# A fused adaLN, H3 convolution and SwiGLU kernel: a second chunk exchanged by PE transposes, three taps on other engines, modulation rows spread through memory, and a new order

## The chip, the cores and the metric

The kernel runs on one core of a Trainium2 chip. The core has a matrix engine (PE), a vector engine (DVE), a scalar engine (ACT), a general engine (POOL, GpSimd) and a queue (SP) that issues the transfers between device memory (DRAM) and on-chip memory (SBUF, 128 partitions). PE writes to PSUM, from which DVE and ACT read. Each engine works through its own instructions in order and waits on semaphores for the others. The metric is the device time of one execution in microseconds (us); lower is better.

## What is computed

Sequence length S = 2048, width D = 512, FFN width F = 1792, all in float32.

```python
def reference(A_q, A_k, A_v, A_shift_k, A_ssm_k, A_ssm_D, B_x, B_w_gate, B_w_up, B_w_down, c, w_mod):
    def _A_ref(q, k, v, shift_k, ssm_k, ssm_D):
        ...
        for t in range(ks):                                   # ks = 4: short causal convolution of k
            k_shift = k_shift + k_pad[:, t:t + S, :] * shift_k[:, ks - 1 - t][None, None, :]
        kv = k_shift * v
        ...
        y_f = kv_f * kf_f[None, :, :, :]                      # long causal convolution by FFT, per channel
        y = irfft2(y_f, ...)[:, 0, :S, :]
        y = y + kv * ssm_D[None, None, :]
        return q * y
    def _B_ref(x, w_gate, w_up, w_down):
        g = _silu(x @ w_gate)
        u = x @ w_up
        return (g * u) @ w_down
    x = A_q
    mod = (_silu(c) @ w_mod).reshape(c.shape[0], 6, 1, -1)
    sa, ca, ga, sb, cb, gb = (mod[:, 0], mod[:, 1], mod[:, 2], mod[:, 3], mod[:, 4], mod[:, 5])
    h = _layernorm(x, axis=-1) * (1 + ca) + sa
    x = x + ga * _A_ref(h, A_k, A_v, A_shift_k, A_ssm_k, A_ssm_D)
    h = _layernorm(x, axis=-1) * (1 + cb) + sb
    x = x + gb * _B_ref(h, B_w_gate, B_w_up, B_w_down)
    return x
```

## The kernel before

**Two halves.** The first half computes the convolution part (A), the second the FFN (B). The FFN is a loop over 14 blocks of 128 hidden columns and two halves of the tokens, with products by a seven-product scheme (`seventh`) in three passes of a high and a low part each. The change leaves the FFN loop as it is, but for the numbers of the buffers that it takes.

**The convolution** is done for four chunks of 128 channels (`c_` = 0 to 3; `b` in the code of the taps). For each chunk:

1. The short convolution of k with k and v laid channel by partition: `tap0` (line 182) makes `u = k * s0`, `tap` (191) adds `k` shifted by t times `s_t`, for t = 1 to 3, on DVE. `tap2` (200) does the same in two instructions for a half of the columns, a product on ACT and a sum on POOL; no call of it stands in the order of before. `times_v` (209) multiplies a quarter of the columns by v, on DVE or POOL.
2. `x_turn` (224) transposes u v on PE, eight 128x128 blocks a call; ACT copies them out.
3. A long Fourier transform in two steps. First step: `x_first` (252) for X = u v and `k_first` or `kx_first` (260, 256) for the filter K (`SS`, to whose first row `skip` (1050) adds the skip term), PE products with the table `raw`, copied out by ACT. Second step: `x2` (342) for X and `prod` (349) for K, whose evacuation is a DVE multiplication by X's result. `inv` (355) is the inverse of the second step, `y_pe` (495) that of the first. `x2`, `prod` and `inv` have a number n: n // 2 is the chunk, so n = 4 and 5 are the halves of chunk 2.
4. Between the two steps partitions and columns have to be exchanged. For X this is `swap_x` (300), a transpose of 32x32 blocks on DVE, number n // 4 being the chunk: 16 calls before the second step, and 12 to 15 once more for chunk 3 behind the inverse. For K of the chunks 0, 1 and 3 it is done on PE: `k_first` multiplies with the operands exchanged and so gives the transposed block, laid by ACT into `KT`, and `k_turn` (280) transposes it back in another grouping. For K of chunk 2 (`put_k`, `get_k`) and for X of the chunks 0 to 2 behind the inverse (`put`, `get`, 308, 312) it goes out to DRAM and back.
5. `y_gate` (507) multiplies `y` with the gate, which `gate_n` (475, ACT), `gate_m` and `gate_a` (485, 489, POOL unless said) make from the normalised x; `add_y`/`add_c` (517, 1067) add to x and take statistics for the second norm; `do_stats` (1064) takes those of the first, a row block at a time, bn_stats and bn_aggr together.

**The modulation.** `mod_part(i)` (382) multiplies silu(c), spread over 32 columns in `csb`, with vector i of `w_mod`, one quarter of the sum to each group of 32 partitions; `mod_bc(i)` (393) adds the four with a selecting matrix `sel` (128x128) and spreads the result over all partitions, for i = 0, 1, 2, 5, and `mod_T` (402) turns 3 and 4 to a column. `mod_mix` (1059) joins 0, 1 and 2, on which `gate_m` and `gate_a` wait.

**The order is written by hand**: lines 1082 to 1601 are one call a line, and each engine, and SP's queue, issues in that order. Functions under `@parts` (66) are split: the first call issues the PE (or first) part, each further call the evacuation that belongs to it. Buffers are numbered by the strings in `HOMES` (32), one digit a request: `ps` are the four double PSUM banks, the others SBUF slots. A request waits until the last reader of that slot's earlier tile is done.

**The end of the first half**: `inv(6)`, `inv(7)`, `swap_x(12..15)`, the last `y_pe`, `y_gate`, `add_c`, then `do_norm2a`, `norm2b` (525), `norm_t` (542, transposes to `nt`), `norm_s` (550), `op_hi`/`op_lo` (610, 619, the high and low parts `B11` and so on) and the first FFN products `gu_pe` (878, tile `g`), with gate weights split by `w8_hi`/`w8_lo` (690, 695).

Of the kernel before, what the change touches and what calls it, by code (L numbers as in the profile page):

```python
# [78 lines left out]
def adaln_h3_swiglu(ctx, tc, q, kT, vT, shk, ssm, dskip, wgu, wdn, c, wmod, e_fwd, e_inv, w_c, out, out_t):  # L79
# [300 lines left out]

    @parts
# [882 lines left out]
    x2(0, 0)
    load_x(0)
    x2(0, 0)
    tap0(3, dve)
    tap(3, 1)
    do_stats(2, 3)
    x_turn(2, 1)  # L1270
    x2(3, 2)
    x2(3, 2)
    prod(0, 2)
    prod(0, 2)
    do_stats(3, 3)
    prod(0, 0)
    gate_n(2, 0)
    x_first(2, 2)
    x_first(2, 2)
    x_first(2, 3)  # L1280
    x_first(2, 3)
    prod(0, 0)
# [1 line left out]
    x_first(2, 1)
    put_k(2)
    load_v(3)
    x_first(2, 0)
    gate_n(3, 2)
    x_first(2, 0)
    swap_x(5)  # L1290
    tap(3, 2)
# [4 lines left out]
    inv(0)
    tap(3, 3)
    x2(3, 1)
    inv(0)
    x2(3, 1)  # L1300
    inv(0)
    x2(3, 0)
    x2(2, 1)
    x2(2, 1)
    prod(3, 2)
    load_ssm(3)
    x2(2, 0)
    gate_n(3, 1)
    prod(3, 2)
    do_stats(1, 0)  # L1310
    x2(3, 0)
    prod(3, 0)
    prod(3, 0)
    x2(2, 0)
    x2(2, 2)
    put(0)
    get_k(2, 0, 1)
    x2(2, 2)
    prod(3, 1)
    prod(3, 1)  # L1320
    do_stats(1, 3)
    prod(2, 0)
    prod(2, 0)
    prod(2, 1)
# [463 lines left out]
```

## Time and profile before

| | us |
|---|---|
| median of 3 runs | 597.17 (595.6 to 598.14) |
| the profiled execution | 597.2 |
| its span, first to last instruction | 595.2 |
| mean granted PE clock | 0.994 of full |

The profile names tiles as the program does: `s` first step, `kt` and `kvt` transposes of K and of u v, `px`, `pk`, `iv` second step and inverse, `xs` results of `x2`, `pb` modulation, `u` and `vt` the short convolution. Busy times of different engines overlap, and a matmul's end is modelled, so that a PE row also holds some waiting. All instructions are recorded through one helper, so they share a line number and are told apart by their tiles. In the chain of work that ended last, each piece was released by the one in front of it.

### The profile page before, as it was taken

Reading aid. Unit: us, or ns where it says so; the run is one execution under the profiler, and the core shown is the slowest. Engines: PE = TensorE matmul, PEld = TensorE weight load, DVE = VectorE, ACT = ScalarE, POOL = GpSimd, SP = SyncE. Lnnn points to the kernel's source line nnn. Section 1 sums busy time; section 2 is a strip of 40 time slices with the busy share of each in tenths; the row PEclk is TensorE's granted clock in tenths of the full one; section 3 lists DMA queues with packets and bytes.
Section 4 is the critical chain, followed back from the end, with each engine's and each line's share of the span. In section 5 each row is a group of like instructions: output and inputs, shape, how many; then the busy total and the mean of one; then the engine's idle time right before and its main releaser. Section 6 shows DMA issues by size and latency. Waiting matters only on the chain.

```text
span 595.2 us, 10149 instructions
## 1 busy us (share of the span) xinstructions
PE 573.3 (96%) x4054; PEld 444.8 (75%) x4054; DVE 475.2 (80%) x625; ACT 297.2 (50%) x444; POOL 321.8 (54%) x243
## 2 busy tenths in 40 slices
PE   6999899999799999999999999999999999999997
PEld 5874436455687788878888888888888888888885
DVE  5999999998987777877868887865577677777875
ACT  3995769785447443444626445354443333333330
POOL 0312133729131597565867794476283838383991
PEclk9999999999989999999999999999999999999999
DMA  8997969888112189174556462065343434343403
GB/s 289 393 391 263 303 173 289 291 262 336 40 35 107 36 314 385 42 254 171 184 241 230 159 253 101 1 244 213 126 160 123 160 123 160 124 159 124 159 2 141
DMA packets 41329, 112.55 MB, mean 189 GB/s; under 512 B 3121, under 2 KB 19649, under 8 KB 35778
## 3 DMA queue, kind: packets, MB, share of 16 engines
q1 hardware_dynamic: 41282, 111.90, 52.6%
q8 instruction: 32, 0.52, 0.3%
q14 instruction: 15, 0.12, 0.1%
HBM read 73.61 MB, written 38.28 MB: 188 GB/s over the span
## 4 chain that ended last, share of the span: by engine, by line
PE 84%; DVE 10%; ACT 2%; issue 2%; DMA 1%; SPq 0%; ACTq 0%; DVEq 0%
PE dn L63 14%; PE b L63 12%; PE a L63 12%; PE c L63 12%; PE dq L63 10%; PE d L63 6%; PE s L63 4%; DVE X L63 4%; PE px L63 3%; PE g L63 3%; PE pk L63 2%; DVE xs L63 2%; PE y L63 2%; PE iv L63 1%; PE kt L63 1%
## 5 line engine op out<-in xcount | busy, mean ns | idle before, releaser
L63 PE MATMUL dn<-wd,acts 128*128 128x512 f32 x336 | 83.7, 391 | 2.3 <-DVE sg L63 1.5
L63 PE MATMUL b<-op,wsum 128*128 128x512 f32 x312 | 79.3, 389 | 0.0
L63 PEld LDWEIGHTS dn<-wd,acts 128*128 128x128 f32 x336 | 62.8, 188 | 16.6 <-ACT acts L63 2.9
L63 POOL TENSOR_TENSOR wa<-ws,wa 128x512 fp32r<-128x512 f32 (+1 forms) x28 | 35.5, 1291 | 70.5 <-ACT wa L63 70.5
L63 PEld LDWEIGHTS b<-op,wsum 128*128 128x128 f32 x312 | 58.5, 188 | 12.4 <-ACT p L63 0.3
L63 PE MATMUL a<-op,wa 128*128 128x512 f32 x228 | 58.1, 390 | 0.0
L63 PEld LDWEIGHTS a<-op,wa 128*128 128x128 f32 x228 | 42.7, 188 | 8.8
L63 DVE TENSOR_TENSOR x<-x,dn 128x512 f32<-128x512 f32 x56 | 37.0, 678 | 12.6 <-PE dn L63 12.5
L63 DVE STREAM_TRANSPOSE X<-X 128x1024 f32<-128x1024 f32 x20 | 44.9, 2304 | 1.7 <-ACT X L63 1.7
L63 POOL TENSOR_TENSOR acts<-sg,acts 128x512 fp32r<-128x512 f32 x16 | 23.2, 1464 | 40.3 <-ACT acts L63 40.3
L63 ACT ACTIVATE sg<-sg 128x512 f32<-128x512 f32 x20 | 12.6, 632 | 63.9 <-DVE sg L63 63.9
L63 POOL TENSOR_TENSOR vt<-u,vt 128x512 f32<-128x512 f32 x12 | 17.0, 1443 | 46.4 <-DVE u L63 38.0
L63 PE MATMUL c<-op,wa 128*128 128x512 f32 x156 | 39.6, 389 | 0.0
L63 PE MATMUL c<-op,wsum 128*128 128x512 f32 x156 | 39.6, 389 | 0.0
L63 PE MATMUL d<-op,wsum 128*128 128x512 f32 x156 | 39.6, 389 | 0.0
L63 POOL TENSOR_TENSOR s<-s,bcs 128x1024 f32<-128x1024 f32 x12 | 28.5, 2395 | 15.5 <-ACT s L63 15.3
L63 POOL TENSOR_TENSOR wsum<-sr,wsum 128x1024 fp32r<-128x1024 f32 x14 | 35.6, 2540 | 0.0
L63 PEld LDWEIGHTS c<-op,wsum 128*128 128x128 f32 x156 | 29.3, 188 | 6.1
L63 PEld LDWEIGHTS d<-op,wsum 128*128 128x128 f32 x156 | 29.3, 188 | 6.1
L63 PEld LDWEIGHTS c<-op,wa 128*128 128x128 f32 x156 | 29.3, 188 | 6.1
L63 DVE SCALAR_TENSOR_TENSOR u<-kt,shk_sb,u 128x1024 f32<-128x1024 f32 (+6 forms) x15 | 28.7, 1916 | 6.0 <-ACT u L63 5.7
L63 ACT COPY p<-a 128x512 f32<-128x512 f32 x26 | 15.4, 591 | 33.3 <-PE a L63 33.3
(169 smaller groups left out, 1344.3 us busy)
## 6 DMA issues: line engine op xcount, KB each, us to landing
kept<-wsum SPq DMA_DIRECT2D x12, 1024.0 KB, 7.7
wsum<-kept SPq DMA_DIRECT2D x12, 1024.0 KB, 6.7
kept<-wa SPq DMA_DIRECT2D x12, 768.0 KB, 6.8
wa<-kept SPq DMA_DIRECT2D x12, 768.0 KB, 4.3
ws<-in_wgu SPq DMA_DIRECT2D x16, 512.0 KB, 5.9
wm<-in_wmod SPq DMA_DIRECT2D x6, 1024.0 KB, 11.4
away<-X SPq DMA_DIRECT2D x3, 2048.0 KB, 11.0
X<-away SPq DMA_DIRECT2D x3, 2048.0 KB, 7.8
```

Of the source, the lines that this page charges most:

```text
L63: return lambda *a, **k: self.tc.keep_in_program_order(f(*a, **k))
```

## The change

Chunk 2 of X is now exchanged on PE, as K of three chunks is: `xk_first(2, ...)` and `xk_turn(2, ...)` take the place of `x_first(2, ...)` and `swap_x(8)` to `swap_x(11)`. Three taps, (2, 3), (3, 2) and (3, 3), go in halves by `tap2` on ACT and POOL; `tap0(3)` goes to ACT. The vectors 0, 1, 5 and 2 of the modulation are computed together by `mod_rows`, each in its group of 32 partitions, copied out once, written to DRAM and read back to all partitions (`mod_out`, `mod_in`). `do_stats` keeps bn_stats alone, and `do_aggr` takes a tile's four aggregations together. `warm(6)` goes, and the order and the buffer numbers are new throughout.

```diff
-    X, K, KT = {}, {}, {}
+    X, K, KT, XK = {}, {}, {}, {}
...
-    @parts
-    def k_first(c_, jq):
+    def by_columns(T, tag, c_, jq, src, o):
 
         ps = banks("s1")
         for jj in range(4):
             for a in range(2):
                 pe.matmul(
-                    ps[:, a, jj * P : (jj + 1) * P], SS[c_][rows(a), 4 * jq + jj], raw[0][rows(a), 4 * jq + jj],
+                    ps[:, a, jj * P : (jj + 1) * P], src[rows(a), o + jj], raw[0][rows(a), 4 * jq + jj],
                     start=True, stop=True,
                 )
         yield
-        if c_ not in KT:
-            KT[c_] = f16(f"kt{c_}", (P, 4, 32, 32))
+        if c_ not in T:
+            T[c_] = f16(f"{tag}{c_}", (P, 4, 32, 32))
         for a in range(2):
             j = J * a + 4 * jq
             act.copy(
-                KT[c_][:, :, j : j + 4, :].rearrange("p g j k -> p j g k"),
+                T[c_][:, :, j : j + 4, :].rearrange("p g j k -> p j g k"),
                 ps[:, a].rearrange("p (j g k) -> p j g k", j=4, g=4),
             )
 
     @parts
-    def k_turn(c_, m):
+    def k_first(c_, jq):
+        return by_columns(KT, "kt", c_, jq, SS[c_], 4 * jq)
+
+    @parts
+    def xk_first(c_, jq):
+        return by_columns(XK, "xk", c_, jq, XT[c_, jq // 2], 4 * (jq % 2))
+
+    def by_turn(T, tag, half, m):
 
         ps = banks("kt").rearrange("p a (k d) -> p (a k) d", k=4)
-        src = KT[c_].rearrange("p g j k -> p (g j) k")
+        src = half.rearrange("p g j k -> p (g j) k")
         for k in range(8):
             pe.transpose(ps[:, k], src[:, :, 8 * m + k], ident)
         yield
-        if c_ not in K:
-            K[c_] = b16(f"K{c_}")
-        act.copy(K[c_][:, 8 * m : 8 * m + 8, :], ps)
+        if tag not in T:
+            T[tag] = b16(f"T{tag}")
+        act.copy(T[tag][:, 8 * m : 8 * m + 8, :], ps)
+
+    @parts
+    def k_turn(c_, m):
+        return by_turn(K, c_, KT[c_], m)
+
+    @parts
+    def xk_turn(c_, m):
+        return by_turn(X, c_, XK[c_], m)
...
+    ROWS = (0, 1, 5, 2)
+
+    @parts
+    def mod_rows():
+
+        ps = bank("pb")
+        for t in range(4):
+            for k, i in enumerate(ROWS):
+                pe.matmul(ps[32 * k : 32 * k + 32], csb[:, t, :], WM[i][:, t, :], start=(t == 0), stop=(t == 3))
+        yield
+        mv_["rows"] = k2([P, D], F32, "rows")
+        act.copy(mv_["rows"], ps)
+
+    def mod_out():
+        w = mv_["away"] = dp.tile([P, D], F32, tag="modr", name="modr")
+        sp.dma_start(w, mv_.pop("rows"))
+
+    def mod_in():
+        w = mv_["away"].rearrange("(k q) d -> k q d", q=32)
+        sp.dma_start(bcs, w[0:3, 0][None].to_broadcast([P, 3, D]))
+        mv_[0], mv_[1], mv_[2] = bcs[:, 0, :], bcs[:, 1, :], k2([P, D], F32, "ga")
+        sp.dma_start(mv_[2], w[3, 0][None].to_broadcast([P, D]))
+
...
-    @parts
-    def mod_bc(i):
-
-        ps = bank(f"pb{i}")
-        pe.matmul(ps, sel, part.pop(i), start=True, stop=True)
-        yield
-        mv_[i] = k2([P, D], F32, "ga") if i == 2 else bcs[:, min(i, 2), :]
-        act.copy(mv_[i], ps)
-
...
-    sel = cp.tile([P, P], F32, name="sel")
+    sel = cp.tile([P, 1], F32, name="sel")
...
+    def do_stats(t, i):
+        if t not in bnq:
+            bnq[t] = cp.tile([P, TB, 1, 6], F32, name=f"bnq{t}")
+        dve.bn_stats(bnq[t][:, i, 0, :], xt[t][:, i, :])
+
+    bnq = {}
+
     @parts
-    def do_stats(t, i):
-        yield from stats(xt[t], f"a{t}", rows_=[i])
+    def do_aggr(t):
+        for i in range(TB):
+            bn[f"a{t}", i] = bnq[t][:, i]
+        yield from stats(xt[t], f"a{t}", True)
```

The order, cut to the places that are spoken of. The start:

```diff
     load_k(0, 0)
-    warm(6)
     load_shk()
-    tap0(0, act, 0)
-    load_e(2)
+    load_d()
+    load_ssm(0, 0)
+    tap0(0, dve, 0)
+    skip(0)
     tap(0, 1, 0)
     tap(0, 2, 0)
     tap(0, 3, 0)
...
+    load_k(0, 1)
     tap0(0, act, 1)
+    load_e(0)
+    k_first(0, 0)
...
     times_v(0, 0)
     load_v(0, 1)
-    times_v(0, 1, pool)
+    times_v(0, 1)
+    load_v(0, 2)
+    x_turn(0, 0)
+    x_turn(0, 0)
+    k_turn(0, 3)
```

The middle as it stands in the new order:

```python
tap2(2, 3, 1)
prod(0, 0)
prod(0, 0)
silu_c()
tap0(3, act)
prod(0, 1)
tap2(2, 3, 1)
...
inv(1)
prod(0, 2)
swap_x(5)
tap2(2, 3, 0)
silu_c()
inv(0)
swap_x(4)
tap2(2, 3, 0)
times_v(2, 3)
inv(1)
times_v(2, 1)
times_v(2, 2, pool)
times_v(2, 0)
load_x(0)
mod_rows()
tap2(3, 3, 1)
tap2(3, 2, 0)
...
tap(3, 1)
inv(1)
inv(0)
k_turn(1, 1)
k_turn(1, 3)
tap2(3, 2, 1)
tap2(3, 2, 1)
tap2(3, 3, 0)
inv(0)
mod_rows()
tap2(3, 2, 0)
...
x_turn(2, 0)
tap2(3, 3, 0)
swap_x(7)
tap2(3, 3, 1)
...
prod(5, 2)
mod_in()
...
put(1)
get(0)
mod_mix()
```

The end of the first half as it stands in the new order:

```python
do_norm2a(0)
y_pe(1, 2, 3)
mod_T(4)
y_pe(3, 0, 1)
do_norm2a(0)
y_gate(1, 2, 3)
w8_hi(0)
do_norm2a(0)
...
y_pe(2, 0, 1)
...
norm_t(0, 0)
norm_s(0, 0)
add_c(1, 2)
y_gate(1, 0, 1)
add_c(1, 3)
add_c(1, 0)
add_c(1, 1)
op_hi("B11")
op_lo("B11", pool)
y_gate(2, 0, 1)
norm_t(0, 1)
...
y_gate(3, 0, 1)
y_pe(2, 2, 3)
y_pe(3, 2, 3)
next_sbuf()
op_hi("B21")
op_lo("B21")
gu_pe(1, 0, 0)
gu_pe(1, 0, 1)
```

More of the change, by code (lines that the diff above doesn't have):

```diff
@@ L1178, in adaln_h3_swiglu @@
-    skip(1, pool)
-    k_first(1, 0)
+    swap_x(0)
+    times_v(1, 1, pool)
+    x_turn(1, 1)
+    load_wc()
     x_turn(1, 0)
-    x_turn(1, 1)
+    x2(1, 0)
+    x_first(1, 3)
+    x_turn(1, 0)
+    load_v(2)
+    skip(1)
+    tap0(2, dve)
+    tap(2, 1)
+    tap(2, 2)
+    x_first(1, 2)
+    x2(1, 0)
     kx_first(2, 1)
-    k_first(1, 0)
-    load_v(2)
+    x_first(1, 2)
     x_first(1, 0)
+    x_first(1, 0)
+    mod_load(0, 5)
+    load_c()
     x_first(1, 1)
     x_first(1, 1)
-    tap0(2, dve)
@@ L1264, in adaln_h3_swiglu @@
[L1264 to L1282, printed above, removed]
-    do_stats(1, 2)
[L1284 to L1291, printed above, removed]
+    tap2(2, 3, 1)
+    prod(0, 0)
@@ new lines, in adaln_h3_swiglu @@
+    prod(0, 0)
+    silu_c()
+    tap0(3, act)
+    prod(0, 1)
+    tap2(2, 3, 1)
+    prod(0, 1)
+    prod(1, 2)
+    prod(0, 2)
+    prod(1, 2)
+    inv(1)
+    prod(0, 2)
+    swap_x(5)
+    tap2(2, 3, 0)
+    silu_c()
+    inv(0)
+    swap_x(4)
+    tap2(2, 3, 0)
+    times_v(2, 3)
+    inv(1)
+    times_v(2, 1)
+    times_v(2, 2, pool)
+    times_v(2, 0)
+    load_x(0)
+    mod_rows()
+    tap2(3, 3, 1)
+    tap2(3, 2, 0)
+    load_x(2)
+    put_k(2)
+    do_stats(3, 3)
+    tap(3, 1)
+    inv(1)
@@ new lines, in adaln_h3_swiglu @@
+    xk_first(2, 2)
+    do_stats(3, 0)
+    xk_first(2, 1)
+    xk_first(2, 3)
+    xk_first(2, 2)
+    xk_first(2, 3)
+    put(0)
+    do_stats(3, 2)
+    do_stats(0, 1)
+    skip(3, pool)
+    do_aggr(3)
+    xk_first(2, 0)
+    xk_first(2, 1)
+    x2(3, 0)
+    x2(3, 2)
+    xk_first(2, 0)
+    do_aggr(3)
+    x2(3, 0)
+    do_stats(2, 2)
+    get_k(2, 2, 3)
+    mod_out()
+    load_x(1)
+    do_stats(0, 0)
+    times_v(3, 2, pool)
+    prod(3, 0)
+    times_v(3, 0, pool)
+    xk_turn(2, 3)
@@ new lines, in adaln_h3_swiglu @@
+    do_aggr(0)
+    prod(3, 0)
+    times_v(3, 1, pool)
+    x2(3, 2)
+    xk_turn(2, 1)
+    get_k(2, 0, 1)
+    xk_turn(2, 1)
+    xk_turn(2, 2)
+    xk_turn(2, 2)
+    do_aggr(3)
+    xk_turn(2, 0)
+    xk_turn(2, 0)
+    xk_turn(2, 3)
+    x2(2, 2)
+    x2(2, 2)
+    x2(2, 1)
+    prod(2, 2)
+    x2(3, 1)
+    times_v(3, 3, pool)
+    x2(2, 1)
+    x2(3, 1)
+    x2(5, 2)
+    x2(2, 0)
+    x2(5, 2)
+    x2(2, 0)
+    prod(3, 2)
+    prod(3, 1)
+    do_aggr(0)
+    do_aggr(0)
+    gate_n(0, 2)
@@ L1292, in adaln_h3_swiglu @@
+    k_first(3, 0)
+    k_first(3, 0)
+    x2(5, 1)
+    k_first(3, 2)
+    x2(4, 1)
+    x2(5, 1)
+    do_stats(1, 0)
+    do_stats(1, 1)
+    do_stats(1, 2)
+    prod(5, 2)
+    prod(5, 2)
+    mod_in()
+    prod(4, 1)
+    x2(4, 1)
+    prod(4, 1)
+    x2(4, 0)
+    x2(4, 0)
+    gate_n(2, 2)
+    gate_n(0, 1)
+    x2(5, 0)
+    x2(5, 0)
+    put(1)
+    get(0)
+    mod_mix()
+    prod(4, 0)
+    prod(5, 0)
+    prod(4, 0)
+    prod(5, 1)
+    gate_m(0, 0)
     do_stats(1, 3)
-    get_k(2, 2, 3)
@@ L1294, in adaln_h3_swiglu @@
-    x_first(2, 1)
+    x_first(3, 1)
+    prod(5, 1)
     gate_n(3, 0)
[L1296 to L1324, printed above, removed]
@@ L1472, in adaln_h3_swiglu @@
     inv(6)
+    prod(7, 1)
+    put(2)
     inv(6)
-    inv(6)
-    gate_n(1, 3)
-    put(2)
-    prod(7, 1)
+    add_c(0, 0)
+    gate_m(1, 0)
     inv(7)
     mod_load(3, 4)
+    inv(6)
+    inv(7)
     mod_part(3)
+    swap_x(12)
+    get(2)
+    y_pe(0, 2)
+    swap_x(13)
+    inv(7)
+    y_gate(0, 2)
+    gate_a(3, 1)
+    gate_a(1, 0)
+    gate_a(2, 0)
     mod_part(3)
-    inv(7)
-    get(2)
     mod_part(4)
     mod_part(4)
-    mod_bc(5)
-    gate_a(2, 1)
+    mod_T(4)
+    swap_x(15)
```

552 lines of the change are left out of this document (231 added, 321 removed).

## The prediction

> **What bounds the kernel now.** I read the page's first part and its clock slices (tenths of full speed), then the busy time of each engine by stretches, then the chain that ended last. The stretches are mine: 16.7 us is where the first 128x128 transposes of K start (`k_turn(0, ...)`), 136.1 where the inverse transform of the last chunk starts (`inv(6)`), 167.7 the first FFN matmul (`g`), 199.5 the first product of the FFN loop. In each row: length, then busy us (and count) of PE, weight loads, DVE, ACT, POOL, then clock and DMA.
>
> ```profile
> span 595.2 us, 10149 instructions
> PE 573.3 (96%) x4054; PEld 444.8 (75%) x4054; DVE 475.2 (80%) x625; ACT 297.2 (50%) x444; POOL 321.8 (54%) x243
> ...
> PEclk9999999999989999999999999999999999999999
> ...
> 16.70:136.10 119.40, 114.78 (x1734) 68.31 (x1734) 116.63 (x113) 96.61 (x117) 40.88 (x26) 1.00 0.90 296
> 136.10:167.70 31.60, 27.80 (x379) 20.55 (x371) 29.51 (x58) 15.76 (x21) 17.40 (x10) 0.90 0.42 167
> 167.70:199.50 31.80, 29.98 (x139) 24.38 (x138) 23.81 (x25) 16.14 (x23) 11.38 (x11) 1.00 0.19 67
> 199.50:595.20 395.70, 391.14 (x1738) 322.67 (x1737) 295.71 (x418) 161.08 (x273) 250.73 (x192) 1.00 0.44 164
> ```
>
> From 199.5 us on PE is busy 391 of 396 us, and the change touches nothing there but buffer numbers: no gain. In the first stretch DVE is busy 116.6 of 119.4 us, so 2.8 us idle, and PE 114.8. PE's figure flatters it, since a matmul that waits is shown as running. Its own pace stands in pieces of the chain without waits and in the groups:
>
> ```profile
> 18.76 0.96 PE kvt L63 x8
> 19.72 0.90 PE kt L63 x8
> ...
> 22.48 10.03 PE s L63 x176
> ...
> L63 PE MATMUL kt<-ident,kt 128*128 128x128 f32 x96 | 12.6, 281 | 2.0 <-ACT kt L63 1.3 <-DVE xs L63 0.6
> L63 PE MATMUL kvt<-ident,vt 128*128 128x128 f32 x64 | 9.3, 291 | 0.4 <-POOL vt L63 0.4
> L63 PE MATMUL pb<-wm,csb 128*32 128x512 f32 x48 | 5.9, 600 | 0.0
> L63 PE MATMUL pb<-part,sel 128*128 128x512 f32 x8 | 4.0, 606 | 0.0
> ```
>
> So 57 ns for a small matmul (10.03/176), 112 for a transpose of K (0.90/8), 120 for one of V, 123 for `pb` from `wm` and 500 for `pb` from `part`. Of the 1734 instructions 96 are `kt`, 64 `kvt`, 32 `wm` (four of six vectors), 6 `part` (three of four), 1536 the rest: 10.8 + 7.7 + 3.9 + 3.0 + 87.6 = **113.0 us of PE work in 119.4**. PE really waits 6.4 us, and the chain shows for whom:
>
> ```profile
> 63.52 2.23 DVE X L63
> 65.75 0.14 issue
> 65.88 1.09 PE px L63 x16
> ...
> 101.06 2.31 DVE X L63
> 103.37 0.14 issue
> 103.50 1.95 PE px L63 x32
> ```
>
> `px` (the forward product) starts when DVE's 32x32 transposes of X end. So in this stretch DVE is the bound and PE stands 6.4 us behind it: whatever leaves DVE, the gain there ends at about 6 us.
>
> **The change part by part.** Durations:
>
> ```profile
> L63 DVE STREAM_TRANSPOSE X<-X 128x1024 f32<-128x1024 f32 x20 | 44.9, 2304 | 1.7 <-ACT X L63 1.7
> L63 DVE SCALAR_TENSOR_TENSOR u<-kt,shk_sb,u 128x2045 f32<-128x2045 f32 x3 | 7.0, 2328 | 0.0
> L63 DVE TENSOR_SCALAR u<-kt,shk_sb 128x2048 f32<-128x2048 f32 x3 | 4.4, 1457 | 0.4 <-DMA kt<-in_kT 0.4
> L63 DVE TENSOR_TENSOR vt<-u,vt 128x512 f32<-128x512 f32 x4 | 3.7, 956 | 0.1
> L63 ACT ACTIVATE u<-kt,shk_sb 128x1024 f32<-128x1024 f32 x2 | 2.3, 1148 | 2.8 <-DMA kt<-in_kT 2.8
> L63 ACT COPY X<-s 128x1024 f32<-128x1024 f32 x16 | 15.4, 1030 | 0.5 <-PE s L63 0.4
> L63 ACT COPY kt<-s 128x512 f32<-128x512 f32 x24 | 12.5, 637 | 2.0 <-PE s L63 2.0
> L63 ACT COPY K<-kt 128x1024 f32<-128x1024 f32 x12 | 12.0, 1024 | 2.2 <-PE kt L63 2.1
> L63 ACT COPY part<-pb 128x512 f32<-128x512 f32 x6 | 3.5, 590 | 4.5 <-PE pb L63 4.5
> L63 POOL TENSOR_TENSOR s<-s,bcs 128x1024 f32<-128x1024 f32 x12 | 28.5, 2395 | 15.5 <-ACT s L63 15.3
> L63 POOL TENSOR_TENSOR vt<-u,vt 128x512 f32<-128x512 f32 x12 | 17.0, 1443 | 46.4 <-DVE u L63 38.0 <-DVE ss L63 8.5
> ```
>
> *DVE, first stretch.* Four exchanges `swap_x(8..11)` go: 4 x 44.9/20 = -9.0. Three taps of 2046 or 2045 columns go: -7.0. `tap0(3)` goes to ACT: -1.5. Two more `times_v` stand on DVE: +1.9; `skip(1)` +0.3. `add_c(0, 0)` moves behind `inv(6)`: -1.6 here, back in the tail. Together -16.9: **DVE 99.7 us**.
>
> *PE.* `xk_turn(2, ...)` adds 32 transposes: 4 x 0.90 = +3.6. `xk_first` issues as many matmuls as `x_first`, with the operands exchanged: 0. `mod_rows` issues the 32 instructions of four `mod_part`: 0. Three `mod_bc` in the stretch go: 6 x 0.5 = -3.0. **PE 113.6 us.** `warm(6)` lies in time in which PE waits for data: 0; the clock is full in the first slices with it; were it half without, matmuls that wait for loads anyway would take double until 15 us.
>
> *ACT.* Six half taps at 1.15 (+6.9), `tap0(3)` at twice that (+2.3), four `xk_turn` copies (+4.0), `xk_first` copies 4 x (2 x 0.52 - 0.96) = +0.3; copies of `part` and, of the same shape, of the broadcasts, 7 x 0.6, go and one `rows` comes (-3.6). **96.6 + 9.9 = 106.5 us**: not the bound, but near it.
>
> *POOL.* Six adds of 128x1024: the trace has that shape as `s<-s,bcs`, 2.4 each, so +14.4; two `times_v` fewer, -2.9; `skip(1)` -0.5; one `w8_lo` from the tail, +2.4: 54 of 119 us. New waits there: `times_v(2, 2)` and so the transposes of V behind the adds of chunk 2; in the new order they stand some 6 us of PE work ahead of `x_turn(2, 0)`. The adds of chunk 3 stand 25 us ahead of theirs. 0; if that cover went, PE would wait for up to one add, 2.4.
>
> *The memory broadcast.* `mod_out` and `mod_in` put three transfers in SP's queue: 0.25 MB out, 0.75 and 0.25 MB back to all partitions. The nearest row, from issue to landing:
>
> ```profile
> rs<-rs SPq DMA_DIRECT2D x4, 256.0 KB, 4.7
> ```
>
> Out and back one after the other, with twice that for the larger one: 10 to 15 us from the copy of the rows to the vectors. Between that copy and `mod_mix`, which needs them, stand over 25 us of DVE and 35 of PE work: 0. On SP's queue `mod_in` stands ahead of `put(1)`, `get(0)`, `get(1)`; `put(1)` waits for `inv(2)` much longer. Without the cover, `mod_mix` would hold DVE, and behind it the `prod` that PE's banks wait for: 5 to 10 us.
>
> *The start.* The first tap moves to DVE; the first loads are in another order.
>
> ```profile
> 11.95 3.91 DVE L63 SCALAR_TENSOR_TENSOR u<-kt,shk_sb,u 128x1024 f32<-128x1024 f32 x3
> ...
> 16.70 2.06 PE L63 MATMUL kt<-ident,kt 128*128 128x128 f32 x16 [1.27 <-ACT kt L63]
> ```
>
> These three taps of the second half of chunk 0 end at 15.9 now. DVE's own half tap (1.46/2) is 0.4 shorter than ACT's 1.15 that they wait for, and some 0.3 of waiting between goes (an estimate), so they end at about 15.2; then two `times_v` (2 x 0.93) come ahead of PE's first transposes, which are V's now: 17.0 for 16.7, +0.3, bounds -1 and +2.
>
> *First stretch, sum.* If PE never waited: 17.0 + 113.6 = 130.6 for 136.1, a gain of 5.5. As bound, DVE was idle 2.8 of 119.4 (2.3%). I give PE the same share: 113.6/0.977 = 116.3, so 133.3: **-2.8**, bounds -5.5 and 0.
>
> *The tail* is a chain: `inv(6)`, ACT's copies, four transposes on DVE, `y`, statistics of x, normalising, transposes `nt`, `g`.
>
> ```profile
> 140.08 6.68 DVE L63 STREAM_TRANSPOSE X<-X 128x1024 f32<-128x1024 f32 x3 [1.75 <-ACT X L63]
> ...
> 153.96 0.17 DVE L63 TENSOR_SCALAR rsb<-mvb 128x4 f32<-128x4 f32 x1
> ...
> 164.08 3.68 PE L63 MATMUL y<-X,ei 128*64 128x128 f32 x32 [1.54 <-ACT hraw L63]
> ...
> 165.00:166.00 1.00, 1.00 (x12) 1.00 (x12) 1.00 (x2) 0.90 (x1) 0.46 (x1) 0.50 0.44 168
> ```
>
> Up to the statistics it is the same instructions, 17.9 us from `inv(6)`. Behind that, the last `y` ran at a clock of 0.50, 32 in 3.68 us, between PE's gaps. The new order leaves two `y` behind `nt` instead of one, the last when DVE has freed its bank (`add_c(1, ...)` and two `y_gate`: some 10 us behind the statistics, 27.9 from `inv(6)`), but `g` starts with a half that needs only `B11` and weights that POOL has split long before. So 27.9 + 1.9 (full clock) to 3.7 (half): 29.8 to 31.6, for 31.6 now: **-0.9**, bounds -1.8 and +1.8 (both `y` at half clock).
>
> *167.7 to 199.5*: PE has 30 of 31.8 us of the same work in a new order: 0, bounds +-1.
>
> Sum: -2.8 - 0.9 = -3.7. The profiled execution took 597.2 (span 595.2 and 2.0 around it), and the median of the runs shown is 597.17, the same: **593.5 us**.
>
> **The rivals.** *PE packs fully* (-5.5 - 1.8): 589.9. For it: the 176 matmuls from 22.5 to 32.5 us show 10 us of PE without a wait even now. Against: ACT at 106.5 now feeds every bank.
>
> *The wait changes its owner.* ACT and PE stand within 7 us of each other and each waits for the other's banks, as PE and DVE do now; if PE keeps waiting 6.4 us, 17.0 + 113.6 + 6.4 = 137.0, and with the tail 597.2. For it: ACT's half taps of chunks 2 and 3 (six, 6.9 us) and `tap0(3)` lie within some 15 us in which PE has inverse transforms and transposes to be copied; against it: ACT still has 10 us of slack.
>
> *Slower: POOL's adds hold DVE.* A DVE instruction with two operands in SBUF that starts beside one of POOL waits for it:
>
> ```profile
> 117.41 4.76 POOL L63 TENSOR_TENSOR s<-s,bcs 128x1024 f32<-128x1024 f32 x2
> ...
> L63 DVE TENSOR_TENSOR s<-s,bcs x4: 1210/1210/3162, 120.1 to 125.5; 128x1024 f32<-128x1024 f32 x4
> ```
>
> The first of the four started at 120.10, POOL's second ended at 122.17, and it took 3.16 for 1.21. Six adds could hold DVE 6 x 2.4 = 14.4 us. DVE has that slack against PE, so a hold costs only where `prod` and PE's banks are queued behind it; it decides when over 5.5 + 0.9 + 3 = 9.4 us of the 14.4 fall there. With all of them PE ends at 130.6 + 14.4 = 145.0: 597.2 + 8.9 - 0.9 = 605. Against: beside the adds the new order has transposes, `prod` (one operand in PSUM) and statistics on DVE, which do not show this. [...]
>
> **How the numbers follow.** Chances: the forecast (591 to 595) 0.50, full packing 0.10, the wait's new owner (595 to 599) 0.30, slower by POOL 0.10 (600 to 605). A measurement of this kernel tells about 0.5% (3.0 us) from no change: faster is below 594.2. Of the forecast 0.47 lies there, with packing 0.57; slower 0.10; the rest, 0.33, within. The range of 589.5 to 598 leaves out 0.04 below and 0.13 above.
>
> **What would show it.** Right: `inv(6)` starts near 133, DVE's busy time up to there near 100, PE's near 114; ACT near 106. Wrong: `px` or `kvt` waiting for ACT or POOL in the table of waits; a DVE instruction of two SBUF operands over 3 us between 45 and 70 us; `mod_mix` or `put` waiting for the broadcast; PE's first transposes after 18 us; a clock of 0.50 for over 7 us in front of `g`.

## The result and the profile after

The changed kernel takes **590.33 us** (median of 5 runs, 589.25 to 592.59) against 597.17 (595.6 to 598.48, now 5 runs): ratio 0.9897, 95% interval 0.9865 to 0.993, 1.0% faster. The forecast was 593.5, in a range of 589.5 to 598. The profiled execution took 592.16 us, so the traces show 5.0 of the 6.8 us between the medians. The five spans lie between 587.5 and 590.8 us, at mean granted clocks between 0.994 and 1.000. Larger samples of the kernel before, taken with the experiments (11 to 21 runs), have medians of 595.6 to 596.9 us, by which the gain is 5.3 to 6.6 us.

The first lines of the changed kernel's page:

```profile
span 590.4 us, 10177 instructions
...
PE 568.6 (96%) x4066; PEld 444.4 (75%) x4066; DVE 456.9 (77%) x621; ACT 304.6 (52%) x451; POOL 330.6 (56%) x246
```

PE is as full as before, in a span 4.8 us shorter; DVE has lost 18 us and ACT and POOL have gained 7 and 9. Where the 4.8 us lie is seen when the trace is cut at the prediction's marks: first transposes, `inv(6)`, first `g`, first product of the loop. The rows by stretches of the changed kernel (length, then busy us and count of PE, weight loads, DVE, ACT, POOL, then clock and DMA); the two below cut the first stretch at 77 us, and the last two show the clock in the tail:

```profile
17.09:133.47 116.38, 114.70 (x1760) 71.54 (x1760) 98.17 (x103) 106.58 (x129) 51.21 (x30) 1.00 0.97 321
133.47:164.54 31.07, 26.58 (x376) 19.69 (x368) 28.54 (x61) 13.90 (x17) 16.14 (x8) 0.95 0.43 167
164.54:194.05 29.51, 29.46 (x138) 24.22 (x137) 24.03 (x26) 17.08 (x24) 9.87 (x10) 1.00 0.14 54
...
49.00:77.00 28.00, 27.27 (x360) 17.19 (x345) 27.85 (x35) 26.42 (x32) 18.49 (x12) 1.00 0.84 279
77.00:133.50 56.50, 56.47 (x942) 29.59 (x941) 42.31 (x52) 51.20 (x62) 25.81 (x14) 1.00 1.01 301
...
142.00:146.00 4.00, 3.30 (x28) 2.39 (x22) 4.00 (x3) 0.58 (x1) 3.20 (x2) 0.92 0.51 150
146.00:150.00 4.00, 3.93 (x48) 3.69 (x44) 2.32 (x7) 0.00 (x0) 0.00 (x0) 0.66 1.01 404
```

And of the kernel before, the first stretch from 49 us on, cut at 77 us too, and the hand-over from the first `g` to the loop, cut at the exact starts:

```profile
49.00:77.00 28.00, 25.36 (x328) 14.34 (x332) 27.62 (x34) 19.96 (x24) 6.37 (x5) 1.00 0.80 243
77.00:136.12 59.12, 57.14 (x939) 29.10 (x923) 58.23 (x59) 47.50 (x58) 27.16 (x15) 1.00 0.89 268
...
167.69:199.32 31.63, 29.80 (x138) 24.21 (x137) 23.64 (x25) 16.16 (x23) 11.30 (x11) 1.00 0.19 67
```

The same cuts for all kernels that were run (from the start of each mark's first matmul; the loop is the span less the start of its first product). The last two columns are the time lost to a granted clock of 0.50 in the first stretch and the tail: the sum of length x (1 - clock) over rows of 2 or 4 us, or over the stretch where its loss is under 4 us. So 1.7 us lost are 3.4 us at half clock; a stretch becomes longer by the loss only where PE sets its pace:

| kernel | start | first stretch | tail | hand-over | loop | lost, first | lost, tail |
|---|---|---|---|---|---|---|---|
| before | 16.70 | 119.42 | 31.57 | 31.63 | 395.9 | 0 | 3.4 |
| changed | 17.09 | 116.38 | 31.07 | 29.51 | 396.4 | 0 | 1.7 |
| `e1_swap2` | 16.30 | 122.77 | 30.67 | 29.48 | 396.2 | 3.4 | 0 |
| `e2_taps_dve` | 16.74 | 125.39 | 30.12 | 29.49 | 395.9 | 1.7 | 0 |
| `e3_both` | 16.52 | 130.69 | 29.39 | 29.53 | 396.1 | 6.8 | 0 |
| `e4_after_dve` | 16.24 | 125.66 | 30.32 | 29.48 | 396.2 | 5.1 | 0 |
| `e5_before_dve` | 15.79 | 131.90 | 31.70 | 31.54 | 395.9 | 6.8 | 3.5 |
| `e6_after_pe` | 16.45 | 118.40 | 33.25 | 29.56 | 396.2 | 0 | 5.1 |
| `e7_before_pe` | 16.47 | 119.67 | 30.70 | 31.67 | 395.9 | 0 | 1.5 |
| `e8_before_sg` | 17.45 | 119.78 | 30.76 | 30.92 | 395.9 | 0 | 1.5 |
| `e9_after_dve_late` | 16.05 | 119.68 | 32.53 | 29.51 | 396.2 | 0 | 3.4 |
| `e10_after_ends` | 15.76 | 115.51 | 34.94 | 29.48 | 396.4 | 0 | 5.1 |
| `e11_before_tap0` | 16.14 | 125.81 | 30.70 | 31.51 | 395.9 | 1.7 | 1.8 |
| `e12_after_ends2` | 16.38 | 115.51 | 32.77 | 30.67 | 396.3 | 0 | 5.1 |

So the change gave, in the trace: start +0.4, first stretch -3.0, tail -0.5, hand-over -2.1, loop +0.5; sum -4.8. How much of that is scatter between executions, the table shows. Seven kernels have the start of the changed one (`changed`, `e1` to `e4`, `e6`, `e9`) and reach the first transposes at 16.05 to 17.09 us, so +0.4 says nothing. Five have the tail of the kernel before (`before`, `e5`, `e7`, `e8`, `e11`): it takes 30.70 to 30.76 us where 1.5 to 1.8 us are lost by the clock, and 31.57 and 31.70 where 3.4 and 3.5 are. The changed kernel, with 1.7 us lost, takes 31.07: its -0.5 is one spell of half clock less, which comes and goes in the old order too, and a gain of the new tail is not shown. The first stretch and the hand-over do repeat: kernels of the old order whose first stretch was left alone (`e7` but for PE's added work, `e8`) have 119.67 and 119.78 us for 119.42, and the hand-over is 31.5 to 31.7 in the old order but for `e8`, which changes it, and 29.5 to 29.6 in the new but for `e12`.

Two things are to be seen in the rows. DVE has 18 us of slack over the first stretch (98.2 of 116.4), but none of it from 49 to 77 us: there it is busy 27.85 of 28.00 us. PE gains all the same: before, it was idle 2.6 us from 49 to 77 us and 2.0 behind 77; now it is idle 0.7 and nothing. And the hand-over holds no wait of PE any more: 29.46 busy of 29.51, where before 1.83 us were missing.

Timeline rows of the changed kernel (start, length, engine, operation; in brackets the idle time before and what ended it), from the start, the first stretch, the tail and the hand-over:

```profile
8.32 0.28 DVE L63 TENSOR_TENSOR ss<-ss,bcs 1x128 f32<-1x128 f32 x1 [2.60 <-DMA ss<-in_ssm]
16.30 2.37 DVE L63 TENSOR_TENSOR vt<-u,vt 128x512 f32<-128x512 f32 x2
16.35 3.45 POOL L63 TENSOR_TENSOR vt<-u,vt 128x512 f32<-128x512 f32 x2 [15.04 <-DVE u L63]
18.73 0.75 PE L63 MATMUL kvt<-ident,vt 128*128 128x128 f32 x4 [0.91 <-DVE vt L63]
...
55.81 1.06 DVE L63 COPY csb<-csil 128x128 f32<-128x128 f32 x1
...
75.88 1.04 DVE L63 SCALAR_TENSOR_TENSOR rsa<-mva,rsa 128x4 f32<-128x4 f32 x1
76.01 2.06 PE L63 MATMUL kt<-ident,xk 128*128 128x128 f32 x16 [0.62 <-DVE xs L63]
...
108.17 4.54 DVE L63 TENSOR_TENSOR s<-s,bcs 128x1024 f32<-128x1024 f32 x2
...
140.80 1.09 PE L63 MATMUL y<-T,ei 128*64 128x128 f32 x16 [0.93 <-DMA T<-away]
141.83 1.07 PE L63 MATMUL pb<-wm,csb 128*32 128x512 f32 x8
142.95 0.33 SPq L63 DMA_DIRECT2D ei<-in_e_inv  x1
145.55 4.38 PE L63 MATMUL y<-X,ei 128*64 128x128 f32 x48
...
188.25 5.97 PE L63 MATMUL dn<-wd,acts 128*128 128x512 f32 x24
```

DVE waits 2.6 us for a load in the middle of the first taps. Its two `vt` stand beside POOL's and take 2.37 us where 2 x 0.93 was reckoned (the same pair took 2.36 in the kernel before), and two sums at 108 us, beside POOL's, 4.54 for 2 x 1.21. Two small operations from 49 to 77 us are long too: the copy to `csb` took 0.18 us in the kernel before, and the operation on `rsa` 0.15 there at 69.18 us, both where POOL was idle. They stand beside POOL's add of 54.79 to 56.79 us and its products from 74.33 us on, so some 1.8 of the 27.85 us (1.06 - 0.18 and 1.04 - 0.15) are likely time in which DVE was held, an estimate from these times. The load of the second table `ei` is issued when the last product of the modulation weights ends (141.83 + 1.07). The last row is the hand-over: 24 `dn` in one run, where the kernel before stopped behind six:

```profile
195.16 4.33 PE L63 MATMUL dn<-wd,acts 128*128 128x512 f32 x18 [1.47 <-DVE sg L63]
```

### The profile page after: what moved, and what is told of

The parts are those of the page before. It is cut to its first block, busy times and chain, and to the rows that moved or that the text cites. A ratio compares the mean times of both kernels' runs of the same rounds, so it can differ in the third digit from the quotient of the medians.

```text
span 590.4 us, 10177 instructions
## 1 busy us (share of the span) xinstructions
PE 568.6 (96%) x4066; PEld 444.4 (75%) x4066; DVE 456.9 (77%) x621; ACT 304.6 (52%) x451; POOL 330.6 (56%) x246
## 4 chain that ended last, share of the span: by engine, by line
PE 84%; DVE 7%; DMA 5%; ACT 2%; issue 1%; SPq 0%; DVEq 0%; ACTq 0%
PE dn L63 15%; PE b L63 12%; PE a L63 12%; PE c L63 12%; PE dq L63 10%; PE d L63 6%; PE s L63 4%; PE g L63 4%; PE px L63 2%; PE pk L63 2%; DMA T<-away 2%; DMA away<-T 2%; PE y L63 2%; DVE u L63 1%; PE nt L63 1%
## 5 line engine op out<-in xcount | busy, mean ns | idle before, releaser
L63 POOL TENSOR_TENSOR wa<-ws,wa 128x512 fp32r<-128x512 f32 (+1 forms) x28 | 34.2, 1243 | 58.3 <-ACT wa L63 58.3
L63 POOL TENSOR_TENSOR s<-s,bcs 128x1024 f32<-128x1024 f32 x12 | 29.9, 2513 | 27.1 <-ACT s L63 26.0
L63 DVE STREAM_TRANSPOSE X<-X 128x1024 f32<-128x1024 f32 x16 | 36.3, 2315 | 2.2 <-ACT X L63 2.2
L63 DVE TENSOR_TENSOR xs<-pk,xs 128x1024 f32<-128x1024 f32 x24 | 28.3, 1215 | 11.5 <-PE pk L63 11.2
L63 DVE TENSOR_TENSOR acc<-acc,dq 128x512 f32<-128x512 f32 x40 | 26.7, 683 | 6.8 <-PE dq L63 6.8
L63 ACT COPY p<-a 128x512 f32<-128x512 f32 x26 | 15.4, 590 | 31.7 <-PE a L63 31.7
```

The costliest lines, as they stand in the source:

```text
L63: return lambda *a, **k: self.tc.keep_in_program_order(f(*a, **k))
```

## The experiments

Each expectation names the theory that was held when it was written; the first one, with the result just seen, was that the sums of work per engine over the whole first stretch decide.

**Parts of the change undone.** The changed kernel with the exchange of X's chunk 2 back on DVE, with the taps back on DVE, and with both; the order of the calls that stay is that of the changed kernel.

```diff
-    xk_first(2, 2)
+    x_first(2, 2)
...
-    xk_turn(2, 1)
-    xk_turn(2, 2)
-    xk_turn(2, 2)
+    swap_x(11)
+    swap_x(10)
```

> The changed kernel with chunk 2 of X exchanged on DVE again (x_first and swap_x(8..11)), all else as changed: DVE 98.4 + 9.0 = 107.4, PE 113.6 - 3.6 = 110.0, ACT 106.8 - 4.3 = 102.5. Bound theory (a stretch costs about its most loaded engine): PE is still the most loaded and lighter, so -2 to +1.5 us: 588.5 to 592. Rival (the exchange on PE is where the gain comes from): +3 or more, 593.5 upwards.

```diff
-    tap2(2, 3, 0)
+    tap(2, 3)
...
-    tap0(3, act)
+    tap0(3, dve)
...
-    tap2(3, 2, 0)
+    tap(3, 2)
...
-    tap2(3, 3, 1)
+    tap(3, 3)
```

> The changed kernel with the three taps and tap0(3) back on DVE: DVE 98.4 + 8.5 = 106.9, ACT 106.8 - 9.1 = 97.7, POOL 51.4 - 14 = 37. Bound theory: PE 113.6 stays the bound, 0 to +2 us: 590 to 592.5. Rival (the taps on ACT and POOL are where the gain comes from): +3 or more. Third (POOL's adds hold DVE): faster, -1 to -3.

> The changed kernel with both back on DVE, in the new order and with the new modulation: DVE 98.4 + 9.0 + 8.5 = 115.9, PE 110.0. Bound theory: DVE is the bound again, the first stretch 2 to 4 us longer: 592.5 to 594.5, inv(6) at 135.5 to 137.5. Rival (the new order carries the gain): within 1 us of the changed kernel.

Measured: 597.49 us, ratio to before 1.0032 (1.001 to 1.0054); 599.11 us, 1.0047 (1.0024 to 1.0069); 604.33 us, 1.0159 (1.0118 to 1.02). Set against the changed kernel's 0.9897 that is 1.35%, 1.50% and 2.62% of 597 us: in the new order the exchange is worth 8.1 us, the taps 9.0, both 15.6. My theory, that only the sums of the engines over the stretch count, fell in all three. Timeline rows of the first and one of the second:

```profile
79.40 1.95 PE L62 MATMUL px<-X,wc 64*32 64x512 f32 x32 [1.75 <-DVE X L62]
...
87.46 1.96 PE L62 MATMUL pk<-T,wc 64*32 64x512 f32 x16 [3.54 <-DVE xs L62]
```

```profile
76.68 3.50 PE L62 MATMUL px<-X,wc 64*32 64x512 f32 x32 [4.62 <-DVE X L62]
```

PE waits again for DVE, as in the kernel before: in the second kernel 4.62 us for transposes of X, in the first 1.75 us for them and then 3.54 for an `xs`, the multiplication that frees PE's bank, which stands behind the four transposes that came back. So the stretch in which DVE sets the pace reaches to 87 us there. A part of these prices is the clock, which fell to 0.50 inside such waits: at 87.4 us in the one of 3.54, at 76.5 in the one of 4.62, and in the third kernel at 74.6 and 95.1 in waits of 4.60 and 4.02 us. So 3.4, 1.7 and 6.8 us are lost in the three first stretches, where the changed kernel loses none. The third kernel's row by stretch, to be read beside the first row of the changed kernel:

```profile
16.52:147.21 130.69, 117.48 (x1728) 69.49 (x1728) 114.44 (x111) 95.24 (x113) 38.64 (x24) 0.95 0.86 287
```

It has 2.2 us less on DVE than the kernel before, and its first stretch is 11.3 us longer than there, at a mean clock of 0.95 (6.8 us lost). So the new order (with the modulation by rows, which stays) is no gain by itself: with DVE's old work in it the kernel is 1.6% slower than before, although it keeps the shorter hand-over. The likely reason is that the order is made for a DVE that is free at certain places; it was not taken apart further.

**Load added** (these four ran first). Sixteen statistics of the first norm made twice (10.9 us more on DVE), and 32 transposes of K's chunk 1 made twice (3.6 us more on PE), each in the kernel before and in the changed one; results stay the same.

```diff
+                if name[0] == "a":
+                    dve.bn_stats(bn[name, i][:, 0, :], xs[:, i, :])
```

> The kernel before with each of the 16 bn_stats of the first norm issued twice into the same place: 16 x 0.68 = 10.9 us more on DVE, nothing else. Bound theory (before, DVE sets the first stretch): DVE 116.6 + 10.9 in a stretch of 119.4, so at least +8 us: 605 (603 to 609), inv(6) at 144 to 147 instead of 136.1. Rival (the order of the work and its waits set the time, not DVE's load): both this and the same edit on the changed kernel cost alike, some 3 to 6 us.

```diff
+        dve.bn_stats(bnq[t][:, i, 0, :], xt[t][:, i, :])
```

> The changed kernel with the same edit, 16 bn_stats more (10.9 us of DVE). Bound theory: DVE 98.4 + 10.9 = 109.3 stays under PE's 113.6, so 0 to +3 us: 590 to 594, inv(6) at 133.5 to 136. Rival: as much as on the kernel before.

```diff
-            pe.transpose(ps[:, k], src[:, :, 8 * m + k], ident)
+            for _ in range(2 if c_ == 1 else 1):
+                pe.transpose(ps[:, k], src[:, :, 8 * m + k], ident)
```

> The kernel before with the 32 transposes of K's chunk 1 issued twice: 32 x 0.112 = 3.6 us more on PE. Bound theory: PE waits 6.4 us for DVE in that stretch, so 0 to +1.5 us: 597 to 598.7. Rival (PE sets the stretch already, as its 96% of busy time says): +3.6.

```diff
-            pe.transpose(ps[:, k], src[:, :, 8 * m + k], ident)
+            for _ in range(2 if T is K and tag == 1 else 1):
+                pe.transpose(ps[:, k], src[:, :, 8 * m + k], ident)
```

> The changed kernel with the same 32 transposes more (3.6 us of PE). Bound theory: PE is the bound now, so +2.5 to +4 us: 593 to 594.3, inv(6) at 136 to 137.5. Rival: as on the kernel before, or nothing.

Measured: DVE's load makes the kernel before 607.82 us (1.0191, 1.0145 to 1.0236) and the changed one 599.69 (1.0068, 1.0034 to 1.0102), 9.4 us over 590.33. PE's load makes the kernel before 596.62 (1.0003, 0.9984 to 1.0022), nothing, and the changed one 593.64 (0.9953, 0.9928 to 0.9977), 3.3 us more, though the intervals of the two just touch. PE's half is as expected in the kernel before: 3.6 us of PE work lie in time in which PE waits (first stretch +0.25 us). In the changed kernel the total is as expected, but `inv(6)` came at 134.85 us for 136 to 137.5: 2.0 of the 3.6 us count in the first stretch. The tail, in which no transpose was added, is 2.2 us longer and loses 3.4 us more by the clock, and that varies between executions: four of the ten runs took 590.6 to 591.8 us at mean clocks of 0.998 to 1.000, five 594.1 to 595.7 at 0.990 to 0.994. So the price of that PE work seems nearer 2 than 3.3 us. DVE's load on the kernel before is as expected in the time; of the 12.5 us by which its first stretch is longer, up to 6.8 are lost by the clock. On the changed kernel DVE's load is a miss: it should hardly have felt it. Its trace says where:

```profile
81.17 3.68 PE L63 MATMUL kt<-ident,xk 128*128 128x128 f32 x16 [6.70 <-DVE xs L63]
```

Ten of the sixteen stand ahead of that `xs`, 10 x 0.68 = 6.8 us, and PE waits 6.70 us, where it waited 0.62 in the changed kernel. The six behind it cost little. So a new theory, in place of the sums, which the undone parts had refuted as well: not the sum, but DVE's chain from 49 to 77 us.

**Where the load stands.** If that is so, load behind 77 us should be free: the last six statistics made three times, 8.2 us. And its counterpart in the kernel before: 4.4 us taken from DVE in the old order.

```diff
-        dve.bn_stats(bnq[t][:, i, 0, :], xt[t][:, i, :])
+        for _ in range(3 if t == 1 or (t, i) in ((2, 0), (2, 1)) else 1):
+            dve.bn_stats(bnq[t][:, i, 0, :], xt[t][:, i, :])
```

> The changed kernel with the last six statistics of the first norm (those that stand behind 77 us) made three times instead of once: 12 more instructions of about 0.68 us, 8.2 us more on DVE, all behind the stretch from 49 to 77 us. Only DVE's time is changed, no result. Theory now (DVE is at its limit only from 49 to 77 us, and idle 18 us in the rest of the first stretch): inv(6) no more than 1 us later than 133.5, 590 to 592.5. Rival (DVE's whole sum of the first stretch counts, as the 10.9 us of the run with all 16 doubled seemed to say at 0.85 us each): 597 to 598.

```diff
-    tap0(1, dve)
+    tap0(1, act)
...
-    tap0(2, dve)
+    tap0(2, act)
...
-    tap0(3, dve)
+    tap0(3, act)
```

> The kernel before with the first tap of chunks 1, 2 and 3 on ACT instead of DVE, order and all else unchanged: DVE 4.4 us less, ACT 6.9 us more. Theory (in the kernel before DVE sets the first stretch, and PE has 6 us to give): inv(6) 3 to 4.4 us earlier than 136.1, 592.5 to 594.5. Rival (work taken from DVE gains only where DVE's chain is, or ACT's copies for PE come later by as much): 596 to 598.

Measured: 595.43 us (0.9972, 0.9954 to 0.999), and 601.27 (1.0079, 1.0059 to 1.01). The first lies between the theories: its first stretch is 3.3 us longer, for 8.2 us of load, though DVE had 14 us of slack behind 77 us. Timeline rows of PE and DVE:

```profile
86.38 1.09 PE L63 MATMUL iv<-xs,wc 32*64 32x512 f32 x8 [0.52 <-DVE xs L63]
...
100.92 2.51 DVE L63 TENSOR_TENSOR xs<-pk,xs 128x1024 f32<-128x1024 f32 x2 [4.87 <-PE pk L63]
...
109.00 1.16 PE L63 MATMUL s<-er,ss 64*128 64x128 f32 x16 [1.06 <-DVE xs L63]
```

The slack could not be moved: a statistic queued in front of an `xs` held PE, 0.52 us at 86 and 1.06 at 109 us, though DVE idled 4.87 us between the two. The second run is the plainest case. DVE has less to do, and the kernel is 4.4 us slower. Timeline rows of ACT, DVE and PE:

```profile
19.93 2.00 ACT L63 ACTIVATE u<-kt,shk_sb 128x2048 f32<-128x2048 f32 x1 [2.33 <-DMA kt<-in_kT]
...
21.97 7.12 DVE L63 SCALAR_TENSOR_TENSOR u<-kt,shk_sb,u 128x2047 f32<-128x2047 f32 x3 [3.45 <-ACT u L63]
...
22.89 1.98 PE L63 MATMUL kvt<-ident,vt 128*128 128x128 f32 x8 [2.83 <-ACT K L63]
```

On ACT the first tap waits 2.33 us for its load, and ACT's copies for PE stand in the queue behind it. So PE stops, and the taps on DVE stop too. Its first stretch is 6.4 us longer than in the kernel before, with 3.2 us less on DVE; up to 1.7 of the 6.4 are half clock, from 22.2 us on, inside the stop, to 25.6.

**The hand-over.** In the kernel before, the product that the last `dn` wait for is put ahead of other work on DVE.

```diff
+    gu_act(1, 1)
     gu_end(0, 1)
...
-    gu_act(1, 1)
```

> The kernel before with one line moved at the hand-over to the FFN loop: DVE's product of gu_act(1, 1) stands ahead of gu_end(0, 1) and the first downs(1) instead of behind them, so that dn's second bank comes free earlier. If the wait of 1.47 us of dn for DVE sg is the lost time there: 167.7 to the loop 31.6 -> 30.3, time 595.9 for 597.2. If the time there hangs on another thing (the splits, the load of wa): no change.

Measured: 594.82 us (0.9991, 0.9971 to 1.001), no difference by the whole time. The stretch itself can be read, since the loop is the same to 0.1 us in the kernels of the old order:

```profile
167.99:198.91 30.92, 29.77 (x139) 24.18 (x138) 24.40 (x25) 16.96 (x24) 11.45 (x10) 1.00 0.20 69
```

30.92 for 31.63: 0.7 of the 2.1 us of the hand-over come with that one step; the wait has changed from DVE's 1.47 us to ACT's:

```profile
181.37 11.21 PE L63 MATMUL g<-op,wg 128*128 128x512 f32 x48 [0.36 <-ACT hraw L63]
...
194.74 4.33 PE L63 MATMUL dn<-wd,acts 128*128 128x512 f32 x18 [0.79 <-ACT acts L63]
```

The rest (that 0.79, the 0.36 for ACT's `hraw`, and 0.3 us in PE's busy time) goes with the other steps of the new order; which of them was not taken apart.

**A better version tried.** The changed kernel with its start put right (the wait of 2.60 us) and its tail in another order. First version:

```diff
-    skip(0)
     tap(0, 1, 0)
     tap(0, 2, 0)
     tap(0, 3, 0)
+    skip(0)
     load_k(0, 1)
-    tap0(0, act, 1)
+    tap0(0, dve, 1)
...
     put(2)
...
+    get(2)
     mod_load(3, 4)
...
+    y_pe(1, 0, 1)
...
     y_pe(0, 2)
...
     mod_part(3)
     mod_part(4)
...
     y_pe(0, 3)
```

> The changed kernel with both ends of its first part put in another order: at the start skip(0) behind the first half taps and tap0(0) of the second half on DVE; in the tail get(2) ahead of the two loads of the modulation weights, y_pe(1, 0, 1) and y_pe(0, 2) ahead of mod_part, y_gate(0, 2) behind the last exchanges. Theory (DVE's wait for the load of ss and ACT's table load hold the start, 32 products y at half clock ahead of y_pe(0, 3) hold the statistics): first transposes 1 to 1.5 us earlier than 17.1, inv(6) to g 29 to 30 us for 31.1, total 587 to 588.5. Rival at the start (the loads set the pace of the first 35 us, whatever the order): no gain there. Rival in the tail (DVE's four exchanges and the loads set it): 31 us as now; both rivals: 590 to 591.

Second version: the start as in the first, `get(2)` behind `mod_load(3, 4)` again, and

```diff
     mod_part(3)
...
+    mod_part(4)
...
+    load_einv2()
+    y_pe(1, 0, 1)
+    y_pe(0, 2)
```

> The changed kernel with the start of the run before last kept (skip(0) behind the first half taps, tap0(0) of the second half on DVE), and another tail: both mod_part right behind inv(7), so that load_einv2, which takes their weights' place, is issued some 2 us earlier than 142.95, and only then y_pe(1, 0, 1) and y_pe(0, 2); mod_load and get(2) in the order of the changed kernel. Theory (y_pe(0, 3) waits for that load, and the load for mod_part(4)): inv(6) at 131.3 as in the run with the first version, inv(6) to g 29 to 30 us for 31.1, total 586.5 to 588. Rival (the loads of these 20 us together set the tail, whatever their order): 31 us, total 588.5 to 590. If the start too gave nothing: 590.

Measured: 594.79 us (0.9976, 0.9958 to 0.9993) and 591.84 (0.9928, 0.9909 to 0.9946). Neither is faster than the changed kernel. The first stretch is 0.9 us shorter in both, and PE's wait of 0.91 us for `vt` at its head is gone. `inv(6)` starts at 131.27 and 131.89 us for 133.47; the other 1.3 and 0.7 are an earlier start, but the start as it was scatters from 16.05 to 17.09 us, so of these (15.76 and 16.38) little is shown to be the new order. The tail gave it back. Rows of the first version's tail, and its clock:

```profile
131.27:166.21 34.94, 28.79 (x376) 22.43 (x368) 28.72 (x61) 14.02 (x17) 16.11 (x8) 0.85 0.46 175
...
146.00:150.00 4.00, 2.96 (x21) 2.66 (x22) 1.13 (x4) 0.00 (x0) 0.00 (x0) 0.51 1.00 398
150.00:154.00 4.00, 4.00 (x35) 3.98 (x37) 2.06 (x11) 1.05 (x1) 1.02 (x1) 0.50 0.04 13
154.00:158.00 4.00, 4.00 (x56) 4.00 (x56) 3.43 (x8) 2.13 (x4) 0.00 (x0) 0.71 0.01 2
```

```profile
147.04 1.97 PE L62 MATMUL y<-X,ei 128*64 128x128 f32 x16 [4.15 <-DMA ei<-in_e_inv]
```

I had taken the cover from a load: `y_pe(0, 3)` needs the second table, the table is asked for only behind `mod_part(4)`, and the 32 products that I moved ahead had covered its way. Timeline rows of the second version, two of the tail and one of the hand-over:

```profile
139.21 0.33 SPq L62 DMA_DIRECT2D ei<-in_e_inv  x1
144.70 1.47 PE L62 MATMUL y<-X,ei 128*64 128x128 f32 x16 [1.80 <-DVE X L62]
...
191.12 4.37 PE L62 MATMUL dn<-wd,acts 128*128 128x512 f32 x18 [1.25 <-DVE x L62]
```

Here the load is asked for 3.7 us earlier and is in time, and DVE's transposes set the pace; but PE stands idle 1.80 us for them, its clock is at half for 10 us in all behind that (5.1 us lost for 1.7 in the changed kernel), and at the hand-over a wait for DVE is back. Its tail loses 3.4 us more by the clock than the changed kernel's; taken off in full that would leave 29.4 us, as expected, but this is an estimate and was not measured.

## Why the prediction came out as it did

**The first stretch: right in size, the reason only half right.** Forecast -2.8 with `inv(6)` at 133.3; it starts at 133.47, and the stretch is 116.38 us for a forecast of 116.3. The engine sums were near: DVE 98.2 for 99.7, ACT 106.6 for 106.5, POOL 51.2 for 54. But "as bound, DVE was idle 2.8 of 119.4" and the step from there to PE's share treat the stretch as one. In the changed kernel DVE is still at its limit from 49 to 77 us and PE in the rest; 6.8 us of load on DVE made PE wait 6.1 us more there, and 8.2 us behind it cost 3.3. The 2.8 us by which the stretch exceeds the 113.6 us of PE work are only in part such waiting: the record has PE idle 1.7 us, 0.9 ahead of 49 us (for `vt`), 0.7 from 49 to 77 us and nothing behind. The step from DVE's idle share to PE's has no support in the traces, so that the stretch came out at 116.38 us for 116.3 is luck, beside the right cause.

**PE's work, the modulation, POOL.** The start of PE's transposes came at 17.1 as forecast (17.0), though held by a load and by `vt` beside POOL, not by the taps alone, and inside a scatter of 1 us. No `put` and no `mod_mix` waits for the broadcast, which took longer than reckoned: some 20 us from the first transfer's issue at 77.67 us to the landing of the last at 97.6 (10 to 15 forecast), 5 us ahead of `mod_mix` at 102.5. The longer times of DVE beside POOL that the slower rival was made of are there, but small: in the two `vt` of the start (0.5 us over the forecast, with PE's wait of 0.91 behind it), in the two small operations of 49 to 77 us (0.9 us each) and in the two sums at 108 us (2.1 us, in DVE's slack). That a DVE instruction with two operands in SBUF waits beside one of POOL has four cases for it in the kernel before: the 3.16 us for 1.21, one of the two `vt` at 15.89 us (2.36 for the pair, 0.69 for one alone), and `rsa` at 88.61 (2.35 for 0.15) and at 105.50 us (1.32). One is against it: the second sum to `bcs` started at 100.39 us, inside POOL's `rsa` of 99.94 to 101.93, and took 0.67. And the copy to `csb`, 1.06 for 0.18 us in the changed kernel, has one operand. What the 1.8 us where DVE is at its limit cost was not tested. Nor was the spreading of the modulation through memory undone by itself, or `warm(6)` put back; what 3.6 us of PE work are worth is known, 2 to 3.3 us in the changed kernel and nothing in the kernel before.

**The tail: -0.9 forecast, -0.5 in the trace, none shown.** The last `y` are at full clock, as the forecast had it at its better end, but the half clock has come earlier, in front of `y_pe(0, 3)`, 3.4 us long instead of 6.8. The forecast read the half clock of one trace as a part of the old order; four more traces of that tail have it from 30.70 us on, and at like loss the new one, 31.07, is no shorter. What the sum left out is PE's wait of 0.93 us for chunk 2 from DRAM.

**The hand-over: the term that was mis-sized.** "PE has 30 of 31.8 us of the same work in a new order: 0, bounds +-1" measured -2.1. The 1.83 us in which PE was not busy stood in the row, and the wait of 1.47 for DVE's `sg` in the trace; I took a new order to leave them. The moved product alone gives 0.7 of it; the other steps were not taken apart.

**The sum**: -3.7 forecast, -5.0 in the profiled execution. That the sum is near is in part errors that cancel: the tail gave less than its term and the hand-over 2.1 us where the sum had nothing. The other 1.8 us to the median stand between runs of the same kernel and are not explained by the one trace. The median is near the rival in which PE packs fully (589.9), but not by it: that rival had the first stretch shorter by 5.5 us, and it became 2.65 earlier at its end. The wait didn't go over to ACT, and DVE's operations beside POOL took some 4 to 5 us more in all (0.5, 1.8 and 2.1), not 14.4.

## What to carry to other kernels

Cut a stretch again after each reckoning: an engine with 15% slack over 116 us can be at 99% for 28 us in the middle, and here a microsecond counted by the instruction it was queued in front of, not by the engine's sum. Before work is moved to an engine with slack, look at what it waits for and at what stands behind it in that queue; 3.2 us of work taken from the limiting engine made this kernel 0.8% slower. A wait of the matrix engine that grew cost more than its length here: inside the 6.70 us of `e4_after_dve` the clock fell to 0.50, and behind them another 2.9 us were lost by it. And before a gain of half a microsecond is read from one trace, see how far that stretch scatters in kernels that share it: here 1.0 us at the start and 1.0 in the tail.

## What the runs showed of the hardware

**Half clock came in pieces.** In the first stretches and the tails of the 14 traces the time lost at a clock of 0.50 is near 0, 1.7, 3.4, 5.1 or 6.8 us, whole pieces of 3.4 us at half clock: one piece in the tail of the changed kernel (145.3 to 148.8 us), two on end in that of the kernel before (161.1 to 167.9). A wait of 1.80 us in the second version of the tail, and waits of 0.93 and 0.70 us among small products in the changed kernel, stood ahead of a fall. Others of that size had none behind them (1.75 us in `e1_swap2`, 1.77 in `e3_both`), so what decides is not shown. With 6.8 us more on DVE (`e4_after_dve`) the clock fell inside the wait of 6.70 us, at about 76.6 us, and stayed at half to 86.9: 6.1 us more of waiting and 2.9 us lost behind it, from 81.2 us on.

**The tail and the clock trade.** The four kernels with a late first stretch (`e1` to `e4`) have tails of 29.4 to 30.7 us at full clock, for 31.07 in the changed kernel with 1.7 us lost: it seems that part of what the first stretch wins is paid back there, though these are single traces. PE's wait of 0.93 us for chunk 2 from DRAM is one piece of it; the rest was not taken apart.
